# Two expert layers after a channel attention: the moving columns of every product read from two halves in turns

## The chip, the cores and the metric

The kernel runs on one core of one Trainium2 chip. The metric is device time in microseconds of one execution. The kernel before takes 1090.8 us, the median of 3 runs (1090.6 to 1090.98 us).

## What is computed

```python
# attention over channels: C = 256 channels, N = 6016 positions
qn = q / norm(q, axis=1); kn = k / norm(k, axis=1)
a  = softmax(kn.T @ qn / tau)          # 256 x 256
x  = v @ a                             # 6016 x 256, the tokens
# first expert layer (256 -> 2048 -> 256)
h = x @ w_in;  g = h - tanh(h);        x = g @ w_out
# second expert layer, of the same sizes
h = x @ w_in2; g = where(h > 0, h, exp(min(h, 0)) - 1);  out = g @ w_out2
```

All inputs and the output are float32.

## The kernel before, in words

The attention comes first: q and k are loaded in chunks, TensorE builds the 256 x 256 matrix S in PSUM (L304), and the softmax of it is folded into the input weights of the first layer (`fold_attention`), so that the first layer reads v itself.

Tokens are the moving columns throughout. They are cut into 12 blocks, 11 of 512 tokens and a last one of 384 (`width`, `blocks`). A tile keeps channels or hidden units on its 128 partitions and the tokens of a block along the free dimension. Every number is split into two float32r parts, hi and lo, and each product of the mathematics becomes three products on TensorE: hi x hi, lo x hi and hi x lo.

For a layer, a block b and one of 8 slices p of the 2048 hidden units, one step does this:

- `emit_h`: the two halves `h[0]` and `h[1]` of the slice, 6 products each, summed in PSUM. The weights stand still and `x_hi`, `x_lo` (tiles `vhi`, `vlo`) move. The products are recorded on the line of the helper `product` (L236); those of the first three steps of layer 1 are issued at L542 in another order of terms.
- `emit_act`: ACT and DVE form g from h, and its two parts `ghi` and `glo`.
- `emit_out`, two steps behind (`LAG = 2`): 12 products that add the slice's share to the two output tiles `o` in PSUM (L702), with `ghi` and `glo` moving. The last block of layer 2 has its own end, `emit_last_out` (L671).
- `emit_evac`, after the 8th slice of a block: ACT copies `o` to the tile `osb` (L716), and a DMA on SP's queue writes it away: for layer 1 to `x_dram`, from which the block is loaded again for layer 2, for layer 2 to the output.

The order of all instructions is written out by hand (`tc.manual_schedule`): `order` runs over slices and blocks, the first two blocks of layer 1 side by side, then block after block, and layer 2 behind layer 1. Weights of both layers are split while the products run (`Converter`: L110 and L127 read every second 32-bit word of a raw tile, L139 reads a contiguous one). PSUM holds two `h` tiles and two `o` tiles.

Of the kernel before, what the change touches and what calls it, by code (L numbers as in the profile page):

```python
# [11 lines left out]
AF = mybir.ActivationFunctionType  # L12
# [4 lines left out]
P = 128  # L17
# [5 lines left out]
def kernel(  # L23
# [17 lines left out]
    nc = tc.nc  # L41
# [20 lines left out]
    win_hi = [wpool.tile([P, KC, F], F32R, name="win_hi0"), None]  # L62
    win_lo = [wpool.tile([P, KC, F], F32R, name="win_lo0"), None]
# [148 lines left out]
    def split_v_scalar(i):  # L212
        _, n = blocks[phases[i][1]]
        raw = v_of[i]
        hi = vpool.tile([P, KC, width], F32R, tag="vhi", name=f"vhi{i}")
        nc.scalar.activation(out=hi[:, :, :n], in_=raw[:, :, :n], func=AF.Copy)
        v_of[i] = (raw, hi)

    def split_v_rest(i, engine):
        _, n = blocks[phases[i][1]]  # L220
        raw, hi = v_of[i]
        lo = vpool.tile([P, KC, width], F32R, tag="vlo", name=f"vlo{i}")
        engine.tensor_tensor(
            out=lo[:, :, :n], in0=raw[:, :, :n], in1=hi[:, :, :n].bitcast(F32), op=ALU.subtract
        )
        v_of[i] = (hi, lo)

    def split_v(i):
        split_v_scalar(i)
        split_v_rest(i, nc.vector)  # L230

    def product(out, terms):

        pairs = [(w[0], x) for w, xs in terms for x in xs] + [(w[1], xs[0]) for w, xs in terms]
        for i, (w, x) in enumerate(pairs):
            nc.tensor.matmul(out=out, lhsT=w, rhs=x, start=(i == 0), stop=(i == len(pairs) - 1))  # L236
# [241 lines left out]
    with tc.manual_schedule():  # L478
# [44 lines left out]
        def emit_h(layer, b, p, last=False):  # L523
            _, n = blocks[b]
            x_hi, x_lo = v_of[layer * NBLK + b]
            h = ps_h.tile([P, 2, 512], F32, tag="h", name=f"h{layer}_{b}_{p}")
            if last:
                h = [h[:, 0], ps_l[0].tile([P, 512], F32, name="h_last")]
            else:
                h = [h[:, 0], h[:, 1], h]  # L530
            if layer == 0 and b + p < 2:

                w_hi, w_lo = [w[0][:, :, 2 * P * p : 2 * P * (p + 1)] for w in (win_hi, win_lo)]
                terms = [(x_hi, w_hi, 0), (x_hi, w_hi, 1), (x_hi, w_lo, 0)]
                terms += [(x_lo, w_hi, 0), (x_lo, w_hi, 1), (x_hi, w_lo, 1)]
                if b == 1:
                    terms = terms[:3] + terms[5:] + terms[3:5]
                elif p == 1:
                    terms = [terms[i] for i in (0, 3, 1, 4, 2, 5)]
                for k, (x, w, c) in enumerate(terms):  # L540
                    for i in range(2):
                        nc.tensor.matmul(  # L542
                            out=h[i][:, :n], lhsT=w[:, c, i * P : (i + 1) * P], rhs=x[:, c, :n],
                            start=(k == 0), stop=(k == len(terms) - 1),
                        )
                return h
            for i in range(2):
                fs = slice((2 * p + i) * P, (2 * p + i + 1) * P)
                product(
                    h[i][:, :n],  # L550
                    [
                        ((win_hi[layer][:, c, fs], win_lo[layer][:, c, fs]), (x_hi[:, c, :n], x_lo[:, c, :n]))
                        for c in range(KC)
                    ],
                )
            return h
# [104 lines left out]
        def emit_last_out(b, p, g):  # L661


            t0, n = blocks[b]
            o = o_of.pop((1, b))
            hi, lo = g
            s = opool.tile([P, 2, width], F32, tag="osb", name="osb")[:, :, :n]
            terms = [(w, x, 0, c) for w, x in ((wout_hi, hi), (wout_lo, hi), (wout_hi, lo)) for c in range(KC)]
            terms += [(w, x, 1, c) for c in range(KC) for w, x in ((wout_hi, hi), (wout_lo, hi), (wout_hi, lo))]
            for w, x, i, c in terms:  # L670
                nc.tensor.matmul(  # L671
                    out=o[c][:, :n], lhsT=w[1][:, 2 * p + i, c * P : (c + 1) * P], rhs=x[:, i],
                    start=False, stop=(i == 1 and x is lo),
                )
            nc.scalar.activation(out=s[:, 0], in_=o[0][:, :n], func=AF.Copy)
            nc.vector.tensor_copy(out=s[:, 1], in_=o[1][:, :n])
            for c in range(KC):
                nc.sync.dma_start(out=outT[c * P : (c + 1) * P, t0 : t0 + n], in_=s[:, c])
# [3 lines left out]
        def emit_out(layer, b, p, g):  # L682
            _, n = blocks[b]
            if p == 0:
                if (layer, b) == phases[-1]:
                    out_stack.close()
                    ps_l.append(ctx.enter_context(tc.tile_pool(name="ps_l", bufs=1, space=PSUM)))
                    o_of[layer, b] = [ps_l[0].tile([P, 512], F32, name=f"o_last{c}") for c in range(KC)]
                else:
                    o = ps_o.tile([P, KC, 512], F32, tag="o", name=f"o{layer}_{b}")  # L690
                    o_of[layer, b] = [o[:, 0], o[:, 1], o]
            o = o_of[layer, b]
            hi, lo = g

            terms = [(wout_hi, hi), (wout_lo, hi), (wout_hi, lo)]
            if layer == b == p == 0:
                terms[1:] = terms[:0:-1]
            for w, x in terms:
                for i in range(2):
                    f = 2 * p + i  # L700
                    for c in range(KC):
                        nc.tensor.matmul(  # L702
                            out=o[c][:, :n],
                            lhsT=w[layer][:, f, c * P : (c + 1) * P],
                            rhs=x[:, i],
                            start=(f == 0 and w is wout_hi and x is hi),
                            stop=(f == 2 * NP - 1 and x is lo),
                        )

        def emit_evac(layer, b, p):  # L710
            if p < NP - 1:
                return
            t0, n = blocks[b]
            o = o_of.pop((layer, b))[2][:, :, :n]
            s = opool.tile([P, 2, width], F32, tag="osb", name="osb")[:, :, :n]
            nc.scalar.activation(out=s, in_=o, func=AF.Copy)  # L716
            if layer == 0:
                nc.sync.dma_start(out=x_dram[b], in_=s)
            else:
                nc.sync.dma_start(  # L720
                    out=outT[:, t0 : t0 + n].rearrange("(k p) t -> p k t", p=P), in_=s
                )
# [15 lines left out]
        nv = 2  # L738

        h0 = emit_h(*order[0])  # L740
        h1 = emit_h(*order[1])
        pend.append((*order[0], emit_act(*order[0], h0, fold_attention(1), late=True, full=True)))
        h2 = emit_h(*order[2])
        pend.append((*order[1], emit_act(*order[1], h1, None, full=True)))
        emit_out(*pend.pop(0))
        pend.append((*order[2], emit_act(*order[2], h2, None, full=True)))
        for s, (layer, b, p) in list(enumerate(order))[3:]:
# [14 lines left out]
            h = emit_h(layer, b, p, last=(s == len(order) - 1))  # L762
# [4 lines left out]
            if done:  # L767
                emit_out(*done)
# [5 lines left out]
            if done:  # L774
                emit_evac(*done[:3])
# [3 lines left out]
            if s == 2 * NP - 2 or (s > 2 * NP and p == 4 and nv < len(phases)):  # L779
                split_v(nv)  # L780
                nv += 1
        emit_out(*pend[0])
        emit_last_out(*pend[1][1:])


# [33 lines left out]
```

## Time and profile before

| what | value |
|---|---|
| median of 3 runs | 1090.8 us (1090.6 to 1090.98) |
| span of the profiled execution | 1088.6 us |
| TensorE busy (PE) | 1082.8 us, 99% |
| weight loads (PEld) | 911.2 us, 84% |
| DVE busy | 841.9 us, 77% |
| ACT busy | 564.0 us, 52% |
| POOL busy | 69.9 us, 6% |
| granted TensorE clock, mean | 1.000 |
| DMA | 54.57 MB, mean 50 GB/s |

The span reaches from the first to the last instruction of the profiled execution; the profile gives no time of that execution beyond it, and the median of the timed runs lies 2.2 us above it. Matmuls are pipelined, so that the durations of products overlap; how fast they follow each other is read from their starts.

### The profile page before, as it was taken

The page shows a single profiled execution, that of the slowest core. Times are in us where ns is not written, and L with a number is a line of the kernel's source. Part 1 is how long each engine was busy: PE and PEld are TensorE (multiplying, and loading weights), DVE is VectorE, ACT ScalarE, POOL GpSimd, SP SyncE. Part 2 cuts the span into 40 slices and gives each one's busy share as a digit, 9 for nine tenths or more (in the row PEclk, how much of TensorE's full clock was granted, in tenths as well). Part 3 has the DMA queues.
Part 4 walks back from the last instruction along what each step waited for, and adds up shares of the span by engine and source line. Part 5 has one row for each costly group of instructions (what it writes and reads, how often), then busy time and mean ns, then how long its engine had stood idle before and what let it go on. Part 6 is the DMA issues. An engine that isn't in the chain of part 4 may idle for free.

```text
span 1088.6 us, 12838 instructions
## 1 busy us (share of the span) xinstructions
PE 1082.8 (99%) x4954; PEld 911.2 (84%) x4954; DVE 841.9 (77%) x926; ACT 564.0 (52%) x665; POOL 69.9 (6%) x65
## 2 busy tenths in 40 slices
PE   9999999999999999999999999999999999999998
PEld 8888888888888888888898888888888888888888
DVE  7899977888776566565657888888878888888887
ACT  7876665444422222222226666666666666666655
POOL 4521211111100000000000000000000000000000
PEclk9999999999999999999999999999999999999999
DMA  9632041222201101101010001011010010110100
GB/s 357 252 117 78 20 136 49 78 84 61 78 1 39 39 1 39 38 2 34 1 40 35 24 16 39 1 39 39 1 39 28 11 39 1 39 39 1 35 20 15
DMA packets 28381, 54.57 MB, mean 50 GB/s; under 512 B 2464, under 2 KB 7840, under 8 KB 28320
## 3 DMA queue, kind: packets, MB, share of 16 engines
q1 hardware_dynamic: 28032, 53.22, 14.5%
q8 instruction: 39, 0.64, 0.2%
q10 hardware_dynamic: 288, 0.52, 0.1%
q14 instruction: 22, 0.18, 0.1%
HBM read 41.42 MB, written 12.32 MB: 49 GB/s over the span
## 4 chain that ended last, share of the span: by engine, by line
PE 98%; DVE 2%; ACT 0%; issue 0%; DVEq 0%; ACTq 0%
PE h L236 46%; PE o L702 45%; PE S L304 4%; PE o_last L702 1%; PE aw L236 1%; DVE g L587 0%; PE warm L316 0%; PE h L542 0%; DVE glo L582 0%; PE o_last L671 0%; DVE cut L139 0%; DVE hz L127 0%; DVE cut L133 0%; DVE cut L146 0%; PE h_last L236 0%
## 5 line engine op out<-in xcount | busy, mean ns | idle before, releaser
L236 PE MATMUL h<-vhi,win_hi 128*128 128x512 f32 (+1 forms) x754 | 290.0, 385 | 0.6 <-DVE g L587 0.6
L236 PE MATMUL h<-vlo,win_hi 128*128 128x512 f32 (+1 forms) x754 | 290.0, 385 | 0.0
L582 DVE TENSOR_TENSOR glo<-g,ghi 128x1024 fp32r<-128x1024 f32 (+1 forms) x191 | 238.3, 1248 | 23.2 <-ACT ghi L616 4.7
L236 PE MATMUL h<-vhi,win_lo 128*128 128x512 f32 (+1 forms) x754 | 228.8, 385 | 0.0
L604 ACT ACTIVATE g<-h 128x1024 f32<-128x1024 f32 (+1 forms) x82 | 82.6, 1008 | 271.1 <-PE h L236 271.1
L702 PE MATMUL o<-ghi,wout_hi 128*128 128x512 f32 (+1 forms) x736 | 195.2, 387 | 0.0
L702 PE MATMUL o<-ghi,wout_lo 128*128 128x512 f32 (+1 forms) x736 | 195.1, 387 | 0.0
L702 PE MATMUL o<-glo,wout_hi 128*128 128x512 f32 (+1 forms) x736 | 195.0, 387 | 0.0
L620 ACT ACTIVATE e<-h 128x1024 f32<-128x1024 f32 (+1 forms) x95 | 96.3, 1014 | 187.6 <-PE h L236 187.6
L605 DVE TENSOR_TENSOR g<-h,g 128x1024 f32<-128x1024 f32 (+1 forms) x82 | 98.3, 1198 | 117.4 <-ACT g L604 117.4
L236 PEld LDWEIGHTS h<-vhi,win_hi 128*128 128x128 f32 x754 | 141.5, 188 | 28.0 <-ACT wout_hi L166 1.0
L236 PEld LDWEIGHTS h<-vlo,win_hi 128*128 128x128 f32 x754 | 141.5, 188 | 27.1
L236 PEld LDWEIGHTS h<-vhi,win_lo 128*128 128x128 f32 x754 | 141.2, 188 | 27.0
L624 DVE SCALAR_TENSOR_TENSOR g<-e,g 128x1024 f32<-128x1024 f32 (+1 forms) x95 | 114.5, 1205 | 60.5 <-ACT e L622 60.3
L702 PEld LDWEIGHTS o<-ghi,wout_lo 128*128 128x128 f32 x736 | 137.8, 188 | 27.6
L702 PEld LDWEIGHTS o<-glo,wout_hi 128*128 128x128 f32 x736 | 137.9, 188 | 27.4
L702 PEld LDWEIGHTS o<-ghi,wout_hi 128*128 128x128 f32 x736 | 137.5, 188 | 26.9
L628 DVE SCALAR_TENSOR_TENSOR g<-h,g 128x1024 f32<-128x1024 f32 (+1 forms) x95 | 114.6, 1206 | 10.2 <-DVE g L624 0.5
L621 ACT ACTIVATE g<-e 128x1024 f32<-128x1024 f32 (+1 forms) x95 | 99.4, 1046 | 3.0
L622 ACT ACTIVATE e<-e 128x1024 f32<-128x1024 f32 (+1 forms) x95 | 99.3, 1046 | 3.0
L632 DVE CAST ghi<-g 128x1024 fp32r<-128x1024 f32 (+1 forms) x95 | 65.0, 685 | 10.1 <-DVE g L628 0.5
L614 DVE CAST ghi<-g 128x1024 fp32r<-128x1024 f32 (+1 forms) x72 | 48.7, 677 | 5.1
(138 smaller groups left out, 668.7 us busy)
## 6 DMA issues: line engine op xcount, KB each, us to landing
qk<-in_q_dram SPq DMA_DIRECT2D x23, 256.0 KB, 5.1
vraw<-in_vT_dram SPq DMA_DIRECT2D x11, 512.0 KB, 5.0
x<-osb SPq DMA_DIRECT2D x11, 512.0 KB, 2.9
vraw<-x SPq DMA_DIRECT2D x11, 512.0 KB, 3.9
out_dram<-osb SPq DMA_DIRECT2D x11, 512.0 KB, 2.9
qk<-in_k_dram SPq DMA_DIRECT2D x21, 256.0 KB, 5.2
raw0in<-in_moe_w_in_dram SPq DMA_DIRECT2D x8, 512.0 KB, 3.7
raw0out<-in_moe_w_out_dram SPq DMA_DIRECT2D x8, 512.0 KB, 3.6
```

What stands on the lines that cost most here:

```text
L236: nc.tensor.matmul(out=out, lhsT=w, rhs=x, start=(i == 0), stop=(i == len(pairs) - 1))
L582: nc.vector.tensor_tensor(out=lo, in0=g, in1=hi.bitcast(F32), op=ALU.subtract)
L604: nc.scalar.activation(out=g, in_=h, func=AF.Tanh)
L605: nc.vector.tensor_tensor(out=g, in0=h, in1=g, op=ALU.subtract)
L614: nc.vector.tensor_copy(out=hi, in_=g)
L620: nc.scalar.activation(out=e, in_=h, func=AF.Relu, scale=-1.0)
L621: nc.scalar.activation(out=g, in_=e, func=AF.Tanh, scale=-0.5)
L622: nc.scalar.activation(out=e, in_=e, func=AF.Exp, scale=-1.0)
L624: nc.vector.scalar_tensor_tensor(out=g, in0=e, scalar=1.0, in1=g, op0=ALU.add, op1=ALU.mult)
L628: nc.vector.scalar_tensor_tensor(out=g, in0=h, scalar=0.0, in1=g, op0=ALU.max, op1=ALU.add)
L632: nc.vector.tensor_copy(out=hi, in_=g)
L702: nc.tensor.matmul(out=o[c][:, :n], lhsT=w[layer][:, f, c * P : (c + 1) * P], rhs=x[:, i], start=(f == 0 and w is wout_hi and x is hi), st ...
```

## The change

The products read the columns of a block in another order. Of n tokens, the moving operand is read as token 0, token n/2, token 1, token n/2 + 1, and so on (`turned`): two halves in turns, one element each. The output is written as pairs that follow each other (`columns`), which is the run of n columns as before. A result column at 2l + s thus belongs to the moving column at s * n/2 + l: the columns are shuffled as two halves of a pack of cards are. Both expert layers have two products each, so that a column is shuffled four times in all. The copy of layer 1's output puts the four shuffles right in advance: it reads 16 neighbours and writes them n/16 elements apart, so that the output of layer 2 comes out in order. No instruction is added, removed or put elsewhere on any engine; the only rows that differ are those 12 copies, of 2 x 32 x 16 elements (in the last block 2 x 24 x 16) where they were runs of 1024 (768).

```diff
--- before.py
+++ after.py
@@ -228,6 +228,13 @@
     def split_v(i):
         split_v_scalar(i)
         split_v_rest(i, nc.vector)
+
+    def turned(x):
+
+        return x.rearrange("p (s l) -> p l s", s=2)
+
+    def columns(out):
+        return out.rearrange("p (l s) -> p l s", s=2)
 
     def product(out, terms):
 
@@ -540,16 +547,20 @@
                 for k, (x, w, c) in enumerate(terms):
                     for i in range(2):
                         nc.tensor.matmul(
-                            out=h[i][:, :n], lhsT=w[:, c, i * P : (i + 1) * P], rhs=x[:, c, :n],
+                            out=columns(h[i][:, :n]), lhsT=w[:, c, i * P : (i + 1) * P],
+                            rhs=turned(x[:, c, :n]),
                             start=(k == 0), stop=(k == len(terms) - 1),
                         )
                 return h
             for i in range(2):
                 fs = slice((2 * p + i) * P, (2 * p + i + 1) * P)
                 product(
-                    h[i][:, :n],
+                    columns(h[i][:, :n]),
                     [
-                        ((win_hi[layer][:, c, fs], win_lo[layer][:, c, fs]), (x_hi[:, c, :n], x_lo[:, c, :n]))
+                        (
+                            (win_hi[layer][:, c, fs], win_lo[layer][:, c, fs]),
+                            (turned(x_hi[:, c, :n]), turned(x_lo[:, c, :n])),
+                        )
                         for c in range(KC)
                     ],
                 )
@@ -669,7 +680,8 @@
             terms += [(w, x, 1, c) for c in range(KC) for w, x in ((wout_hi, hi), (wout_lo, hi), (wout_hi, lo))]
             for w, x, i, c in terms:
                 nc.tensor.matmul(
-                    out=o[c][:, :n], lhsT=w[1][:, 2 * p + i, c * P : (c + 1) * P], rhs=x[:, i],
+                    out=columns(o[c][:, :n]), lhsT=w[1][:, 2 * p + i, c * P : (c + 1) * P],
+                    rhs=turned(x[:, i]),
                     start=False, stop=(i == 1 and x is lo),
                 )
             nc.scalar.activation(out=s[:, 0], in_=o[0][:, :n], func=AF.Copy)
@@ -700,9 +712,9 @@
                     f = 2 * p + i
                     for c in range(KC):
                         nc.tensor.matmul(
-                            out=o[c][:, :n],
+                            out=columns(o[c][:, :n]),
                             lhsT=w[layer][:, f, c * P : (c + 1) * P],
-                            rhs=x[:, i],
+                            rhs=turned(x[:, i]),
                             start=(f == 0 and w is wout_hi and x is hi),
                             stop=(f == 2 * NP - 1 and x is lo),
                         )
@@ -713,10 +725,16 @@
             t0, n = blocks[b]
             o = o_of.pop((layer, b))[2][:, :, :n]
             s = opool.tile([P, 2, width], F32, tag="osb", name="osb")[:, :, :n]
-            nc.scalar.activation(out=s, in_=o, func=AF.Copy)
             if layer == 0:
+
+                nc.scalar.activation(
+                    out=s.rearrange("p k (q u) -> p k u q", q=16),
+                    in_=o.rearrange("p k (u q) -> p k u q", q=16),
+                    func=AF.Copy,
+                )
                 nc.sync.dma_start(out=x_dram[b], in_=s)
             else:
+                nc.scalar.activation(out=s, in_=o, func=AF.Copy)
                 nc.sync.dma_start(
                     out=outT[:, t0 : t0 + n].rearrange("(k p) t -> p k t", p=P), in_=s
                 )
```

## Rows read from the trace of the kernel before

**Rows 1.** The page: span; engines, busy us (share of the span), instructions.

```profile
span 1088.6 us, 12838 instructions
...
PE 1082.8 (99%) x4954; PEld 911.2 (84%) x4954; DVE 841.9 (77%) x926; ACT 564.0 (52%) x665; POOL 69.9 (6%) x65
```

**Rows 2.** The page: chain that ended last, by engine and by line.

```profile
PE 98%; DVE 2%; ACT 0%; issue 0%; DVEq 0%; ACTq 0%
PE h L236 46%; PE o L702 45%; PE S L304 4%; PE o_last L702 1%; PE aw L236 1%; DVE g L587 0%; PE warm L316 0%; PE h L542 0%; DVE glo L582 0%; PE o_last L671 0%; DVE cut L139 0%; DVE hz L127 0%; DVE cut L133 0%; DVE cut L146 0%; PE h_last L236 0%
```

**Rows 3.** Busy time of each engine in two stretches of layers 1 and 2.

```profile
core 0: us, PE busy (x) PEld busy (x) DVE busy (x) ACT busy (x) POOL busy (x), PEclk, DMA share, GB/s
...
300.00:500.00 200.00, 200.00 (x884) 165.68 (x883) 123.97 (x125) 47.65 (x50) 2.23 (x3) 1.00 0.06 22
...
700.00:900.00 200.00, 200.00 (x884) 165.67 (x883) 164.76 (x152) 125.44 (x121) 0.00 (x0) 1.00 0.08 27
```

**Rows 4.** PE in order of time: start, us, line, products merged (512 columns).

```profile
302.24 1.07 PE L702 MATMUL o<-ghi,wout_hi 128*128 128x512 f32 x4
303.15 1.07 PE L702 MATMUL o<-ghi,wout_lo 128*128 128x512 f32 x4
304.06 1.07 PE L702 MATMUL o<-glo,wout_hi 128*128 128x512 f32 x4
304.96 0.39 PE L236 MATMUL h<-vhi,win_hi 128*128 128x512 f32 x1
```

**Rows 5.** PE in order of time, in the last block (384 columns).

```profile
566.08 0.85 PE L702 MATMUL o<-ghi,wout_hi 128*128 128x384 f32 x4
...
568.16 0.39 PE L236 MATMUL h<-vhi,win_hi 128*128 128x512 f32 x1
```

**Rows 6.** Groups by line and form: count | busy us, mean ns | idle before.

```profile
L236 PE MATMUL h<-vhi,win_hi 128*128 128x512 f32 x692 | 269.3, 389 | 0.6 <-DVE g L587 0.6
...
L702 PE MATMUL o<-ghi,wout_hi 128*128 128x512 f32 x704 | 188.4, 389 | 0.0
...
L236 PE MATMUL h<-vhi,win_hi 128*128 128x384 f32 x62 | 20.7, 334 | 0.0
...
L702 PE MATMUL o<-ghi,wout_hi 128*128 128x384 f32 x32 | 6.9, 335 | 0.0
...
L702 PE MATMUL o_last<-ghi,wout_hi 128*128 128x384 f32 x28 | 6.0, 334 | 0.0
...
L542 PE MATMUL h<-vhi,win_hi 128*128 128x512 f32 x12 | 3.9, 417 | 0.0
...
L671 PE MATMUL o_last<-ghi,wout_hi 128*128 128x384 f32 x4 | 1.3, 355 | 0.0
...
L236 PE MATMUL h_last<-vhi,win_hi 128*128 128x384 f32 x2 | 0.7, 334 | 0.0
```

**Rows 7.** Groups by line and form: stepped reads (L110, L127), unstepped (L139).

```profile
L139 DVE SCALAR_TENSOR_TENSOR cut<-hz,cut 128x512 uint32<-128x512 uint32 x16 | 11.1, 691 | 0.5
...
L110 ACT ACTIVATE sq<-raw1out 128x256 f32<-128x256 f32 x16 | 6.9, 429 | 0.0
...
L127 DVE SCALAR_TENSOR_TENSOR hz<-sq,raw0in 128x512 f32<-128x512 f32 x8 | 5.4, 680 | 0.0
...
L110 ACT ACTIVATE sq<-raw0out 128x512 f32<-128x512 f32 x8 | 5.3, 661 | 0.0
```

**Rows 8.** PE in order of time: the attention's plain float32 products.

```profile
22.07 1.89 PE L304 MATMUL S<-qk 128*128 128x256 f32 x8
23.61 0.47 PE L304 MATMUL S<-qk_hi 128*128 128x256 f32 x1
```

**Rows 9.** In order of time: a copy of layer 1's output and its neighbours.

```profile
370.44 1.03 ACT L716 ACTIVATE osb<-o 128x1024 f32<-128x1024 f32 x1 [1.69 <-PE o L702]
...
371.50 0.33 SPq L718 DMA_DIRECT2D x<-osb  x1
...
373.16 1.03 ACT L604 ACTIVATE g<-h 128x1024 f32<-128x1024 f32 x1 [1.69 <-PE h L236]
```

## The prediction

> **What bounds the kernel now.** I read the page's busy times first, then the chain that ended last, then stretches, then single products. TensorE (PE) is busy 1082.8 us of a span of 1088.6 us [rows 1], and the chain of work that ended last is 98% TensorE, 91% of the span in the two lines that this change edits, L236 and L702 [rows 2]. The reader should see that no other engine gives the pace: in the stretch 300 to 500 us TensorE is busy for all 200.00 us with 884 products, ACT only 47.65 us, and in 700 to 900 us the same 884 products take the same 200.00 us although ACT works 125.44 us and DVE 164.76 us there [rows 3]. [...]
>
> So the time is the number of products times their pitch, and the pitch is read from starts, not from the durations, which overlap. Twelve products of 512 columns start at 302.24 us and the next group at 304.96 us [rows 4]: 2.72 / 12 = 226.7 ns. Twelve of 384 columns start at 566.08 us and the next group at 568.16 us [rows 5]: 2.08 / 12 = 173.3 ns. [...]
>
> How many columns go through the edited lines: of 512 columns there are (692 + 12 + 704) x 3 = 4224 products, of 384 columns (62 + 2 + 32 + 28 + 4) x 3 = 384 [rows 6]; each of these rows stands for three alike, one for each pair of parts. That is 4608 products and 2.310 million columns: 2.310 million x 0.417 ns = 963 us of streaming and 4608 x 13.3 ns = 61 us of fixed parts, 1024 us of the 1088.6. The other 64 us (attention, folds, the tail) are not touched.
>
> **The change, part by part.** No instruction is added, removed or moved; only access patterns change.
>
> *The output of each product.* It is written as pairs that follow each other, which is the same run of 512 addresses as before. Cost: nothing.
>
> *The copy of layer 1's output.* It runs 12 times on ACT, and now writes in steps of 32 words (24 in the last block). The row takes 1.03 us for 1024 elements a partition, about one element in a nanosecond [rows 9]. From below it stays at that; from above I let it double, +1.0 us each, 12 us of ACT in all. What hides it: the next ACT instruction starts at 373.16 us, 1.69 us after the copy has ended, because it waits for TensorE [rows 9]; and the transfer behind the copy fills a buffer that is read again only in layer 2. Without that cover it would be 12 us; with it, nothing.
>
> *The moving columns.* Column 0 of each half, column 1 of each half, and so on: consecutive columns lie 256 words (192 in the last block) apart, where before they were neighbours. The trace has no product that reads its columns in this way, so I bound it from rows. From below: a column costs the same wherever it lies, +0 us. From above: the nearest engine that picks single words out of a stepped source is ACT squaring every second word of the raw weights, 429 ns for 256 and 661 ns for 512 elements [rows 7], (661 - 429) / 256 = 0.906 ns for one more element. At that price the columns cost 2.310 million x (0.906 - 0.417) ns = 1130 us more. In between lies the nearest slower product of TensorE itself: the plain float32 products of the attention, 8 of 256 columns from 22.07 us to 23.61 us [rows 8], 192.5 ns each or 0.752 ns a column with the fixed part in it, which would add 2.310 million x 0.752 ns - 1024 us = 713 us. That row reads neighbours, in another format; it only shows a rate that is neither of the ends.
>
> I take the value nearest to ACT's row. ACT spends 0.906 ns on a word, and TensorE alone takes a four-byte word each 0.417 ns. The simplest reading is that it is fed two neighbouring words by one access. With the halves in turns no access holds two words that are wanted next, and each column costs an access of its own: two column times, 0.833 ns. That adds 2.310 million x 0.417 ns = 963 us. A step of two words alone costs nothing here: on DVE the operation with one stepped source takes 680 ns and its like with none 691 ns [rows 7]. So this rests on the distance between consecutive words, which no row shows. [...]
>
> **The sum.** Span 1088.6 + 963 + 0 + 0 = 2051.6 us. The median of the runs shown, 1090.8 us, is 2.2 us above the span of the profiled execution, so I add 2.2: 2054 us. If reading is the slower side, the fixed 13.3 ns between products may hide behind it, 61 us less: 1993 us. The likeliest case's own range is 1985 to 2065 us. Other engines have room: DVE's 842 us and ACT's 564 us [rows 1] stay as they are while TensorE's time nearly doubles.
>
> **The rivals.**
>
> *The columns cost what they did (no change).* [...] It also covers the case that the pattern is put back into one run when built. [...] Time: 1091 us. [...]
>
> *Faster.* This is one mechanism at one place: the 13.3 ns between two products. If they are the start of the moving read (waiting for the first words of a fresh run), two runs opened together could overlap that start. The price is up to 61 us, so 1029 us at the end and about 1060 us if half goes; it decides as soon as streaming itself stays at 0.417 ns. For it: the fixed part is the same at 384 and 512 columns, as a start would be. Against it: it could as well be the change of weights, which the edit leaves alone, since each product loads its own.
>
> *Slower by part of it.* A reader that covers some of the distance, at a rate between one and two column times. The float32 row's rate gives 1091 + 713 = 1804 us; the case holds everything from 1093 to 1985 us. Against it: such rates have no reason in the rows but that one.
>
> *Slower still.* At ACT's price of a word: 1091 + 1130 = 2221 us; at four column times for a column, 1091 + 3 x 963 = 3980 us. For it: nothing but that no row bounds the price of a distant word; against it: no engine in these rows takes more than about 1 ns for one.
>
> **How the numbers follow.** Likeliest case 0.41, part of it 0.11, slower still 0.08: slower 0.60. No change 0.24. Faster 0.16. About 0.2%, 2.2 us, is what a measurement of this kernel can tell from no change. The point is the likeliest case, 2054 us. The likeliest case's range alone holds too little; to leave no more than 2 in 10 out, the range has to take in the unchanged case, and it reaches down to the end of the faster one, 1029 us, and up to 2065 us; outside lies only "slower still".
>
> **What would show it.** Right: in 300 to 500 us some 455 to 470 products where there were 884, at a granted clock of 1.00; starts of 512-column products 427 to 440 ns apart, of 384 columns 320 to 333 ns; float32 products and folds before and between as they were; ACT's and DVE's waits for TensorE grown by about the whole difference. Wrong: a pitch of 226.7 ns in the same stretch (no change), or one of 213 to 226 ns (the fixed part shrinks). The two sizes tell a price per column from one per product. The copies of layer 1 may grow to about 2 us each with nothing waiting for them; if TensorE stands idle at the start of a block, my cover for them is wrong.

## The result and the profile after

The changed kernel takes 1041.87 us, the median of 4 runs (1041.52 to 1042.26), against 1090.85 us before: a ratio of 0.9552 with a 95% interval of 0.9539 to 0.9566. It is 49 us faster, where the prediction had 963 us more as the likeliest case.

The page after, in the lines that answer to those of [rows 1] and [rows 2] (L243 and L714 are L236 and L702 of before):

```profile
span 1039.7 us, 12840 instructions
...
PE 1032.8 (99%) x4954; PEld 912.2 (88%) x4954; DVE 842.7 (81%) x926; ACT 586.9 (56%) x665; POOL 69.8 (7%) x65
...
PE 97%; DVE 2%; ACT 1%; issue 0%; DVEq 0%; ACTq 0%
```

TensorE is still the bound, with the same 4954 products. ACT works 22.9 us longer and DVE as long as before. The two stretches of [rows 3], after:

```profile
300.00:500.00 200.00, 200.00 (x928) 175.12 (x928) 126.91 (x123) 54.90 (x50) 0.73 (x1) 1.00 0.08 26
...
700.00:900.00 200.00, 200.00 (x929) 175.13 (x928) 173.37 (x160) 130.03 (x126) 0.00 (x0) 1.00 0.08 27
```

There are 928 and 929 products where there were 884, at the same granted clock of 1.00. So the products follow each other more closely, in both layers alike. The starts tell how much more; TensorE in order of time, 512 columns and, in the last block of layer 1, 384 columns, as in [rows 4] and [rows 5]:

```profile
287.10 1.03 PE L714 MATMUL o<-ghi,wout_lo 128*128 128x512 f32 x4
287.96 1.03 PE L714 MATMUL o<-glo,wout_hi 128*128 128x512 f32 x4
288.82 0.38 PE L243 MATMUL h<-vhi,win_hi 128*128 128x512 f32 x1
...
536.25 0.33 PE L243 MATMUL h<-vhi,win_hi 128*128 128x384 f32 x1
...
540.14 0.33 PE L243 MATMUL h<-vhi,win_hi 128*128 128x384 f32 x1
```

Eight products of 512 columns from 287.10 to 288.82 us are 215.0 ns each within the rounding of the rows, and 24 of 384 columns from 536.25 to 540.14 us are 162.1 ns each. Read from the starts of all products of a size, with the longest and the shortest twentieth of the distances left aside, as all starts below are unless said, the means are 215.9 and 162.5 ns where they were 226.7 and 173.6 ns. Divided by size: 53.4 ns for 128 columns is 0.417 ns a column, about as before (53.1 ns, 0.415 ns a column). What has changed is the part that a product pays whatever its size: at 0.417 ns, 512 columns are 213.5 ns, which leaves 226.7 - 213.5 = 13.2 ns before and 215.9 - 213.5 = 2.4 ns after. 4224 x 10.8 + 384 x 11.1 ns = 50 us; the span fell by 48.9 us, and the other 1.1 us is TensorE standing idle 6.9 us in all instead of 5.8 us.

Two groups answer to [rows 7] and [rows 9] in another way than they stood there (groups by line and form; L730 is the stepped copy of layer 1's output, L737 the plain one of layer 2's):

```profile
L730 ACT ACTIVATE osb<-o 128x1024 f32<-128x1024 f32 x11 | 22.4, 2038 | 11.0 <-PE o L714 11.0
...
L737 ACT ACTIVATE osb<-o 128x1024 f32<-128x1024 f32 x11 | 11.1, 1012 | 0.0
...
L110 ACT ACTIVATE sq<-raw0out 128x512 f32<-128x512 f32 x8 | 6.7, 834 | 0.0
...
L127 DVE SCALAR_TENSOR_TENSOR hz<-sq,raw0in 128x512 f32<-128x512 f32 x8 | 6.3, 792 | 0.0
```

The stepped copy takes twice as long, 2038 ns. And two instructions that the change does not touch are slower: ACT's read of every second word 834 ns instead of 661 ns, DVE's 792 ns instead of 680 ns.

### The profile page after: what moved, and what is told of

Its sections match the earlier page's. It is cut to its first block, busy times and chain, and to the rows that moved or that the text cites. A ratio compares the mean times of both kernels' runs of the same rounds, so it can differ in the third digit from the quotient of the medians.

```text
span 1039.7 us, 12840 instructions
## 1 busy us (share of the span) xinstructions
PE 1032.8 (99%) x4954; PEld 912.2 (88%) x4954; DVE 842.7 (81%) x926; ACT 586.9 (56%) x665; POOL 69.8 (7%) x65
## 4 chain that ended last, share of the span: by engine, by line
PE 97%; DVE 2%; ACT 1%; issue 0%; DVEq 0%; ACTq 0%
PE h L243 46%; PE o L714 45%; PE S L311 4%; PE aw L243 1%; PE o_last L714 1%; DVE g L598 0%; DVE glo L593 0%; PE warm L323 0%; DVE cut L139 0%; DVE hz L127 0%; DVE cut L146 0%; PE o_last L682 0%; DVE win_lo L258 0%; DVE cut L133 0%; ACT g L597 0%
## 5 line engine op out<-in xcount | busy, mean ns | idle before, releaser
L243 PE MATMUL h<-vhi,win_hi 128*128 128x512 f32 (+1 forms) x754 | 282.5, 375 | 0.7 <-DVE g L598 0.7
L243 PE MATMUL h<-vlo,win_hi 128*128 128x512 f32 (+1 forms) x754 | 282.4, 375 | 0.0
L243 PE MATMUL h<-vhi,win_lo 128*128 128x512 f32 (+1 forms) x754 | 221.0, 375 | 0.0
L714 PE MATMUL o<-ghi,wout_hi 128*128 128x512 f32 (+1 forms) x736 | 187.2, 377 | 0.0
L714 PE MATMUL o<-glo,wout_hi 128*128 128x512 f32 (+1 forms) x736 | 187.2, 377 | 0.0
L714 PE MATMUL o<-ghi,wout_lo 128*128 128x512 f32 (+1 forms) x736 | 187.1, 377 | 0.0
L243 PEld LDWEIGHTS h<-vhi,win_hi 128*128 128x128 f32 x754 | 142.5, 189 | 19.8 <-ACT wout_hi L166 1.1
L243 PEld LDWEIGHTS h<-vlo,win_hi 128*128 128x128 f32 x754 | 142.5, 189 | 18.6
L243 PEld LDWEIGHTS h<-vhi,win_lo 128*128 128x128 f32 x754 | 141.7, 189 | 18.5
L714 PEld LDWEIGHTS o<-ghi,wout_lo 128*128 128x128 f32 x736 | 138.5, 189 | 18.9
L714 PEld LDWEIGHTS o<-glo,wout_hi 128*128 128x128 f32 x736 | 138.5, 189 | 18.9
L714 PEld LDWEIGHTS o<-ghi,wout_hi 128*128 128x128 f32 x736 | 138.0, 189 | 18.5
```

The lines of the kernel that those rows point to most:

```text
L714: nc.tensor.matmul(out=columns(o[c][:, :n]), lhsT=w[layer][:, f, c * P : (c + 1) * P], rhs=turned(x[:, i]), start=(f == 0 and w is wout_hi ...
```

## The experiments

The theory that the runs led to is an order of the measured starts: the products behave as if two readers shared the moving columns, one the columns at places 0, 2, 4, ... of the pattern and the other those at 1, 3, 5, ..., each with one line of 16 bytes (four float32 words) open, and as if a change of line cost time. Neighbours in order give each reader two words of a line (0 and 2, 1 and 3), at 226.7 ns a product of 512 columns; two halves in turns give it four in a row, at 215.9 ns. That four words make a line is read from the runs as well. Were it two, the one run that is not in order (0, 2, 1, 3; 226.7 ns) would use each line up as the change does; were it eight, neighbouring lines (0, 4, 1, 5; 215.9 ns) would take four words of each, as neighbours in order do (226.7 ns). No run shows the readers or the lines themselves. The first four runs below were made with other explanations in mind, and the theory was drawn from them; the runs from neighbouring lines on put it to the test. The rivals: what counts is the distance from one word to the next; two long runs opened together overlap a start; any pattern that is no single run works; the halves must lie far apart; the fixed part belongs to the weights.

All patterns below change the two functions that the products share, `turned` and, to match it, `columns` (and leave layer 1's copy plain, unless said). The diffs are excerpts: each shows the line that decides, without those that follow from it. A row of TensorE with x4 holds four products, so that from its start to the start of the next row it is four distances.

**Two neighbours from each half.**

```diff
-        return x.rearrange("p (s l) -> p l s", s=2)
+        return x.rearrange("p (s l w) -> p l s w", s=2, w=2)
```

> The two halves are read in turns, two neighbouring columns each instead of one; the reordering of layer 1's copy is left out, so the tokens of a block come out in another order. If what counts is the way from one word to the next (a new 16-byte line at every column), the fixed part of a product comes back: starts 227 ns apart and about 1091 us. If any pattern that jumps takes it away, 216 ns and about 1042 us. If a start of the read is overlapped by two open runs, 216 ns too.

Measured: 1567.12 us against 1091.26 us; starts 333 ns apart. TensorE in order of time:

```profile
470.63 1.51 PE L714 MATMUL o<-ghi,wout_hi 128*128 128x512 f32 x4
471.96 1.51 PE L714 MATMUL o<-ghi,wout_lo 128*128 128x512 f32 x4
```

None of the three outcomes: two open runs are not enough, and it is far worse than neighbours in order. In the theory one reader now alternates between two lines at every word (0, 256, 2, 258).

**Four neighbours from each half.** The same with `w=4`.

> As before it, with four neighbouring columns each, one whole 16-byte line; tokens come out in another order. Distance from word to word: 227 ns, about 1091 us, since three of four steps stay in a line. Two open runs or any jumping pattern: 216 ns, about 1042 us.

Measured: 1194.19 us; starts 250 ns apart. TensorE in order of time:

```profile
481.95 1.17 PE L714 MATMUL o<-ghi,wout_hi 128*128 128x512 f32 x4
482.95 1.17 PE L714 MATMUL o<-ghi,wout_lo 128*128 128x512 f32 x4
```

Again slower than before, so two open runs do nothing by themselves. A reader uses two words of a line (0, 2), as before, but jumps 1 KB to the next.

**One run, not in order.**

```diff
-        return x.rearrange("p (s l) -> p l s", s=2)
+        return x.rearrange("p (l b c) -> p l c b", b=2, c=2)
```

> Columns 0, 2, 1, 3 of every four: no step leaves the 16-byte line before it is used up, and there is one run through the tile, but no two columns that follow each other are neighbours in order; tokens come out in another order. Two open runs: 227 ns, about 1091 us, since there is only one. New line at every column: 227 ns. Any pattern that isn't one run of neighbours: 216 ns, about 1042 us.

Measured: 1091.2 us against 1091.26 us; starts 227 ns apart, no change at all. That no columns which follow each other are neighbours does not matter, so a pattern that merely isn't one run is out. Here too a reader uses two words of a line (0, 1 for one and 2, 3 for the other), now neighbours, and two are not enough.

**Even columns, then odd ones.**

```diff
-        return x.rearrange("p (s l) -> p l s", s=2)
+        return x.rearrange("p (l s) -> p s l", s=2)
```

> All even columns, then all odd ones: a step of two words, two hits on each line, one run at a time; tokens come out in another order. Two open runs: 227 ns, about 1091 us. New line at every column: between 216 and 227 ns. Any pattern that isn't one run of neighbours: 216 ns, about 1042 us.

Measured: 2100.54 us; starts 451 ns apart, and all three expectations failed. TensorE in order of time:

```profile
605.43 1.99 PE L714 MATMUL o<-ghi,wout_hi 128*128 128x512 f32 x4
607.24 1.99 PE L714 MATMUL o<-ghi,wout_lo 128*128 128x512 f32 x4
```

Four products take 1.81 us. The halved rate of the prediction exists, but here at a step of two words, where two columns in a row still lie in one line. With two readers it has a reason: 0, 4, 8 and 2, 6, 10 bring each of them a new line at every word.

**One word from each of two neighbouring lines.**

```diff
-        return x.rearrange("p (s l) -> p l s", s=2)
+        return x.rearrange("p (b s l) -> p b l s", s=2, l=4)
```

> Columns 0, 4, 1, 5, 2, 6, 3, 7 of every eight: one word each from two lines that are neighbours, so a new line at every column as in the change, but 16 bytes away instead of 1 KB; the copy of layer 1 is as before, tokens come out in another order. If columns are taken in pairs and each of the two has a reader of its own that keeps one line open, the fixed part is gone as in the change: 216 ns, about 1042 us. If the two halves have to lie in different parts of the memory, 227 ns or more, 1091 us or above.

Measured: 1041.4 us against 1090.83 us; starts 215.9 ns apart. TensorE in order of time:

```profile
156.36 1.03 PE L714 MATMUL o<-ghi,wout_hi 128*128 128x512 f32 x4
157.23 1.03 PE L714 MATMUL o<-ghi,wout_lo 128*128 128x512 f32 x4
```

The whole gain, with the two lines 16 bytes from each other and runs of four words: that the halves must lie far apart is out, and so is a start of two long runs. Two readers with an open line each had told it.

**Four quarters in turns.**

```diff
-        return x.rearrange("p (s l) -> p l s", s=2)
+        return x.rearrange("p (s l) -> p l s", s=4)
```

> Four quarters in turns, one element each; tokens come out in another order. Two readers with one open line each: every reader changes its line at every word, as with pairs: 333 ns or more, about 1570 us or above. Any number of open runs: 216 ns, about 1042 us.

Measured: 1339.43 us; starts 283 ns apart. TensorE in order of time:

```profile
404.11 1.30 PE L714 MATMUL o<-glo,wout_hi 128*128 128x512 f32 x4
405.25 0.45 PE L243 MATMUL h<-vhi,win_hi 128*128 128x512 f32 x1
```

The direction is that of two readers (four open runs would have kept the gain), the size is not: 283 ns instead of 333 ns or more. Going back and forth between two lines (283 ns here, 333 ns with two neighbours from each half) costs less than going on to a new one (451 ns with even and odd columns), which the theory does not say.

**The weights, stepped** (kernel before; each output tile takes every second channel):

```diff
-                            lhsT=w[layer][:, f, c * P : (c + 1) * P],
+                            lhsT=w[layer][:, f].rearrange("p (m c) -> p c m", c=KC)[:, c],
```

> The kernel before, with the weights of layer 2's and layer 1's second products read in steps of two words (channels 0, 2, 4, ... for one output tile, 1, 3, 5, ... for the other, so the output's channels come out mixed); the moving columns are read as before. If the fixed 13 ns are the two reads of TensorE meeting in the memory, these products' starts move away from 227 ns, up to 240 ns (about 1120 us), since their weights take twice the lines; the first products of each layer stay at 227 ns. If they are the start of the moving read, 227 ns and about 1091 us.

Measured: 1105.29 us. The second products start 233.3 ns apart at 512 columns, 6.6 ns more than before; at 384 columns 173.2 ns, as before. TensorE in order of time:

```profile
173.02 1.09 PE L702 MATMUL o<-ghi,wout_hi 128*128 128x512 f32 x4
173.95 1.09 PE L702 MATMUL o<-ghi,wout_lo 128*128 128x512 f32 x4
```

It moves in the way of the first branch, within the 240 ns that it allowed, but at 512 columns alone; that branch had no reason for a difference between the sizes. So how the weights are read bears on the distance of the products. That the two reads meet in the memory is not shown.

**Half the weights in one term** (kernel before):

```diff
+                        m = P // 2 if w is wout_lo else P
                         nc.tensor.matmul(
-                            out=o[c][:, :n],
-                            lhsT=w[layer][:, f, c * P : (c + 1) * P],
+                            out=o[c][:m, :n],
+                            lhsT=w[layer][:, f, c * P : c * P + m],
```

> The kernel before, with 64 instead of 128 columns of weights in one of the three terms of the second products (hi with the low part of the weights), whose other half is left out of the sum. If the fixed 13 ns come from reading the weights, the groups with 64 columns start about 5 ns closer (221 to 222 ns), about 1087 us in all; if from the start of the moving read, 227 ns as the others and 1091 us.

Measured: 1096.56 us against 1090.83 us, slower, not faster. The loads of 64 columns take 134 ns instead of 188 ns, and the groups with them start no closer (TensorE in order of time):

```profile
331.09 1.07 PE L703 MATMUL o<-ghi,wout_hi 128*128 128x512 f32 x4
332.00 1.08 PE L703 MATMUL o<-ghi,wout_lo 128*64 128x512 f32 x4
332.92 1.09 PE L703 MATMUL o<-glo,wout_hi 128*128 128x512 f32 x4
333.84 0.39 PE L236 MATMUL h<-vhi,win_hi 128*128 128x512 f32 x1
```

0.92 us for the four with half the weights, 0.91 us for those ahead. Over the whole trace the products with half the weights take 230.0 ns to the next start and the full ones right behind them (`glo`, `wout_hi`) 231.6 ns, the others of 512 columns 226.5 to 226.7 ns: 704 x 3.3 + 704 x 4.9 ns = 5.8 us, which is the whole loss. So both branches fail: the fixed part does not shrink with the weights that are read, and why less to load makes these products longer stays open.

**Sixteen columns, two runs of 32 bytes.** With `l=8` in the pattern of neighbouring lines, four shuffles cancel, so that no copy need be reordered.

> Columns 0, 8, 1, 9, ... 7, 15 of every sixteen: two runs of 32 bytes in turns. Four such shuffles of sixteen give the old order back, so layer 1's output is copied as before and nothing is left out. Two readers, one open line each: 216 ns between the starts and 1041.4 us, as with adjacent lines, at least as fast as the change, since ACT's stepped copy of 2.0 us is gone. If the changed kernel still lost something to that copy, or to the slower stepped reads of ACT and DVE beside it, 1 us less than the change or more.

Measured: 1041.77 us, the median of 5 runs, against 1090.80 us (ratio 0.9551, interval 0.9537 to 0.9564); starts 215.9 ns apart. The same gain as the change's, without its copy; nothing is won by leaving the copy out. The reads that the change made slower are as before (groups by line and form):

```profile
L127 DVE SCALAR_TENSOR_TENSOR hz<-sq,raw0in 128x512 f32<-128x512 f32 x8 | 5.4, 680 | 0.0
...
L110 ACT ACTIVATE sq<-raw0out 128x512 f32<-128x512 f32 x8 | 5.4, 671 | 0.0
```

**The stepped copy alone**, on the kernel before:

```diff
-            nc.scalar.activation(out=s, in_=o, func=AF.Copy)
             if layer == 0:
+                nc.scalar.activation(
+                    out=s.rearrange("p k (q u) -> p k u q", q=16),
+                    in_=o.rearrange("p k (u q) -> p k u q", q=16),
+                    func=AF.Copy,
+                )
```

> The kernel before with the stepped copy of layer 1's output alone, moving columns as before (tokens come out in another order). Hidden behind the products: 1091 us, no difference from before, copies of 2.0 us. If it were on the path: up to 12 us more.

Measured: 1090.72 us against 1090.80 us, ratio 0.9999 (0.9990 to 1.0008), with copies of 2117 ns. Hidden.

**Only the hi parts in turns.** The lo parts' columns are read as neighbours:

```diff
-                    rhs=turned(x[:, i]),
+                    rhs=turned(x[:, i]) if x is hi else plain(x[:, i]),
```

> The hi parts' columns are read from two halves in turns, the lo parts' as neighbours (so the lo parts are added to other tokens; copy of layer 1 as before). If the fixed part belongs to the product whose columns are read (its own start or its own running out of lines), a product of hi lasts 216 ns and one of lo 227 ns to the next start: 2/3 of the gain, about 1058 us. If it is lost at the start of the product behind one that could not read ahead, the step from lo to hi is 227 ns and from hi to lo 216 ns as well; if at the start of the product that reads as neighbours, the step from hi to lo is the 227 ns.

Measured: 1064.05 us, a little over half of the gain and not the two thirds that were expected. TensorE in order of time, where lo products (`vlo`, `glo`) stand between hi products:

```profile
301.34 0.59 PE L246 MATMUL h<-vhi,win_lo 128*128 128x512 f32 x2
301.77 1.03 PE L717 MATMUL o<-ghi,wout_hi 128*128 128x512 f32 x4
302.64 1.03 PE L717 MATMUL o<-ghi,wout_lo 128*128 128x512 f32 x4
303.50 1.09 PE L717 MATMUL o<-glo,wout_hi 128*128 128x512 f32 x4
304.43 0.38 PE L246 MATMUL h<-vhi,win_hi 128*128 128x512 f32 x1
304.64 0.39 PE L246 MATMUL h<-vlo,win_hi 128*128 128x512 f32 x1
304.88 0.38 PE L246 MATMUL h<-vhi,win_hi 128*128 128x512 f32 x1
```

From a hi product to a lo product 0.21 us (304.43 to 304.64), from a lo product to a hi product 0.24 us (304.64 to 304.88); four hi products take 0.87 us, four lo products 0.93 us. Over the whole trace a hi product takes 215.5 ns to the next start and a lo product 231.5 ns, 4.8 ns more than where all products read neighbours; 1408 x 4.8 ns = 6.8 us is about what is missing, and its cause stays open. The loss lies behind the recorded start of a product that reads neighbours and ahead of the next start, not ahead of its own: a wait ahead of the recorded start is out. A wait for the first words behind it would look the same in this trace. The results of hi and lo products are written alike, through `columns`, so it is not the pattern on the writing side that takes the fixed part away.

**The folds too.** The change left the attention's products as they were. On the kernel with sixteen, the attention's folds now read their 256 columns in turns, and ACT and DVE put them back in order as they leave PSUM:

```diff
-            out=win_hi[0][:, m, fs], in_=ps[:, : 2 * P], func=AF.Copy, scale=rsum[:, m : m + 1]
+            out=halves(win_hi[0][:, m, fs]), in_=pairs(ps[:, : 2 * P]), func=AF.Copy, scale=rsum[:, m : m + 1]
```

> As the run with sixteen, and the attention's folds into the weights read their 256 columns in turns too, with the copies out of PSUM putting them back in order. 96 products by 11 ns: 1 us less, 1040.4 us, if their copies stay hidden; no gain or up to 2 us more if ACT's and DVE's stepped writes there delay the first products.

Measured: 1041.77 us (ratio to before 0.9550, 0.9537 to 0.9563), no better than without. The folds' products start 112 instead of 120 ns apart (medians), but their copies grow from 472 to 716 ns on ACT and from 476 to 677 ns on DVE, and from 45 to 70 us TensorE is busy for 22.81 us where it was 23.29 us: it waits for them. Two of the waits stand between a fold and a first product of layer 1: from the start of the one to the start of the other it is 0.50 us where it was 0.19 us, and 0.41 us at an earlier place.

Two causes were left for the two readers: how often each changes its line, or that both ask for the same one when neighbours are read in order.

**A new line at every word, never shared.**

```diff
-        return x.rearrange("p (s l) -> p l s", s=2)
+        return x.rearrange("p (s l r) -> p r l s", s=2, r=4)
```

> Column 0 of every line of the two halves in turns, then column 1 of every line, and so on: each of the two readers gets a new line at every word, as with the even and odd columns (451 ns), but the two columns of a pair lie in different lines; tokens come out in another order. If what counts is how often a reader changes its line, about 451 ns, 2100 us. If it is that both ask for the same line, far less: 283 ns as with quarters, about 1340 us, or 216 ns.

Measured: 2100.73 us; starts 451 ns apart, to the nanosecond those of even and odd columns, where the line was shared. TensorE in order of time:

```profile
605.65 1.99 PE L714 MATMUL o<-ghi,wout_hi 128*128 128x512 f32 x4
607.46 1.99 PE L714 MATMUL o<-ghi,wout_lo 128*128 128x512 f32 x4
```

**A new line at every second word, never shared** (blocks of 512; half of the words of each of the two channel groups):

```diff
+        flat = x[:, :, :n].rearrange("p k t -> p (k t)")
+        return flat.rearrange("p (s l q w) -> p q l w s", s=2, q=2, w=2)[:, c]
```

> Blocks of 512: the two readers take two neighbouring words of a line and go on to the next line, one in the first and one in the second channel group of the tile (so the products read words of both groups, and half of the words of a tile; the values are others). Each reader changes its line at every second word, as it does when neighbours are read in order (227 ns), but never shares the line with the other. If the fixed part comes from the changes of line, 227 ns, about 1091 us; if from the shared line, 216 ns, about 1045 us. The last block of 384 reads neighbours: 173 ns.

Measured: 1091.42 us; starts 226.7 ns apart, as before. TensorE in order of time:

```profile
302.78 1.07 PE L720 MATMUL o<-ghi,wout_hi 128*128 128x512 f32 x4
303.68 1.07 PE L720 MATMUL o<-ghi,wout_lo 128*128 128x512 f32 x4
```

Sharing the line does not matter; how often a reader changes it does. Here the two readers also open two lines of their own at the start of each product, as in the change, and the fixed part is still there: it is not an overlapped start that takes it away. A single reader that sees all columns one after another is out as well: this pattern goes to another line at every column, and neighbours in order at every fourth, with the same 227 ns.

All patterns in one table, sorted by how many words of a line each of the two readers takes before it changes it:

| pattern (first columns) | words to a line | starts, 512 columns | starts, 384 columns |
|---|---|---|---|
| the change: 0, 256, 1, 257 | 4 | 215.9 ns | 162.5 ns |
| neighbouring lines: 0, 4, 1, 5 | 4 | 215.9 ns | 162.5 ns |
| sixteen: 0, 8, 1, 9 | 4 | 215.9 ns | 162.5 ns |
| before: 0, 1, 2, 3 | 2 | 226.7 ns | 173.6 ns |
| one run, not in order: 0, 2, 1, 3 | 2 | 226.7 ns | 173.6 ns |
| new line at every second word, not shared | 2 | 226.7 ns | (neighbours) |
| four from each half: 0 to 3, 256 to 259 | 2, with jumps | 250 ns | 191 ns |
| quarters: 0, 128, 256, 384 | 1, back and forth | 283 ns | 204 ns |
| two from each half: 0, 1, 256, 257 | 1, back and forth | 333 ns | 247 ns |
| even and odd: 0, 2, 4, 6 | 1, new | 451 ns | 340 ns |
| new line each, not shared | 1, new | 451 ns | 340 ns |

Among the patterns with one word before a change, the time follows how many words of a line a reader uses in all before it is done with it: four in the quarters, two in the pairs, one in the last two rows (283, 333 and 451 ns). This order was read from the table; no run was made for it.

## Why the prediction was wrong

**What bounds the kernel: right.** TensorE's pitch set the time, and its split into 0.417 ns a column and 13.3 ns a product was the right one. [rows 4, 5] give it: (226.7 - 173.3) / 128 = 0.417 ns a column, and 226.7 - 512 x 0.417 = 13.2 ns a product, which leaves the sum's 61 us for 4608 products as they are. That this part is the same at each size takes a third one: the attention's folds, 256 columns, start 119.9 ns apart before, 119.9 - 256 x 0.417 = 13.1 ns. The difference after is 10.8 ns a product at 512 columns and 11.1 ns at 384. One row was misread on the way: the plain float32 products of [rows 8] start 216 ns apart inside their group, 0.84 ns a column; the 192.5 ns came from dividing up to the start of the next row, which is recorded 28 ns behind the last of the eight. The sum did not use it, only the rival "slower by part of it" did.

**The moving columns: the step that failed.** "With the halves in turns no access holds two words that are wanted next, and each column costs an access of its own: two column times, 0.833 ns." That took one reader that gets two neighbouring words at a time. The runs show another thing in its place: alternate columns behave as two streams, and what decides is how many words of a 16-byte line each takes before it goes to another: one on each new line gives 451 ns a product of 512 columns, two 226.7 ns, four 215.9 ns. The change gives each stream whole lines, so it reads with fewer changes than before, not with more, and a product became 10.8 ns shorter instead of 213 ns longer. The doubled rate is real, 451 ns, but belongs to streams that go to a new line at every word. No row of before could tell this, since every product there read neighbours; [rows 7], a step of two words at no cost on DVE, says nothing of TensorE, where the same step doubles a product (451 ns for 226.7 ns).

**The rival "faster": right in place, wrong in mechanism.** It priced the 13.3 ns at up to 61 us and gave 1029 us at the end and 1060 us halfway; 10.8 of the 13.2 ns went at 512 columns, 50 us in all. Its mechanism, two runs opened together that overlap a start, fell: neighbouring lines with runs of four words gain as much, four words from each half lose, and two lines opened together with two words taken from each keep the whole fixed part (226.7 ns). "It could as well be the change of weights" fell as it stood, since the change leaves the weights alone and half of them shortens nothing; that their read and the moving one bear on each other is not out. Its chance of 0.16 was too low for a fixed part of which no row showed the cause.

**No change: wrong.** From before to the change the price of a column stayed at about 0.417 ns (53.1 and 53.4 ns for the 128 columns between the two sizes), but the fixed part did not stay. Nor is that the price of every pattern: with even and odd columns the 128 columns take 451 - 340 = 111 ns, 0.87 ns a column.

**The copy of layer 1: right.** It was bounded at double its time, took 2.04 us, and cost nothing: a ratio of 0.9999 with the copy alone.

**Still open.** Why the fixed part is there with two words to a line. It is no price for each change of line: the change takes 10.8 ns from a product of 512 columns and 11.1 ns from one of 384, though the longer one has a third more lines. So the two readers order the patterns, but do not explain a loss that is the same at both sizes. Nor is it known where in the product the 11 ns are lost, whether the load of the weights has a part in it (stepped weights take a product from 226.7 to 233.3 ns, half the weights shorten none: 230.0 ns), why going back and forth between two lines costs less than new ones (283 and 333 ns against 451 ns), or why stepped weights cost 6.6 ns at 512 columns alone.

## What to carry to other kernels

Where TensorE sets the pace with float32r products, read the distance between starts at two sizes: a part that does not depend on the size (13.2 ns here) need not be the weights. Let alternate columns come from two different 16-byte lines and use each line up (0, 8, 1, 9, ...: 215.9 ns where neighbours took 226.7 ns); sixteen columns shuffled four times come back in order by themselves, and no copy has to undo it. Keep away from a step of two words on the moving side, and from any pattern that gives each of the two streams a new line at every word: both doubled the time of a product here (451 ns).

## What the runs showed of the hardware that was not expected

- A step of two float32 words in the moving columns doubles a product (451 instead of 227 ns), while a jump of 1 KB at every column makes it shorter (215.9 ns).
- Under two of TensorE's reading patterns other engines were slower. With halves 1 KB apart, in the change, ACT's reads of every second word took 834 instead of 661 ns and DVE's 792 instead of 680 ns; with four words from each half 864 and 788 ns. With the same gain from runs of 32 bytes they took 671 and 680 ns. The 1 KB alone doesn't do it: with two words from each half, as far apart, they took 683 and 679 ns. The cause was not looked for. Reads of neighbours did not change (L139: 691 ns before and after the change).
- An ACT copy out of PSUM that writes 32 words apart takes 2038 ns where the plain one takes 1012 ns.
